# One transfer in place of two or three: x pieces, stage 2's load and its store in a Fourier mixing and routing kernel

## The chip, the cores and the metric

The kernel runs on one core of a Trainium2 chip. The metric is the device time of one execution in microseconds (us); a figure for a kernel is the median of several executions. All numbers below come from such executions, from one execution taken by the hardware profiler, or from the order of instructions in the built program.

A core has engines with instruction streams of their own: TensorE (PE in the profile, PEld for its weight loads), VectorE (DVE), ScalarE (ACT), GpSimd (POOL) and SyncE (SP), which computes nothing and here issues transfers. ACT and POOL issue transfers besides their computation. An engine takes its instructions in order, so one that waits holds up those behind it on that engine.

## The reference

The input is x with 8 batches of 2496 rows of 256 channels (float32). Each batch is filtered along its rows by a Fourier transform; then each of the 19968 rows goes through the two-layer network of one of 8 experts, which its token id selects.

```python
def _attn_ref(x, filt_r, filt_i):            # x (8, 2496, 256), filters (1249, 256)
    X = np.fft.rfft(x, axis=1)
    Y = X * (filt_r + 1j * filt_i)[None, :, :]
    return np.fft.irfft(Y, n=x.shape[1], axis=1).astype(np.float32)

def _moe_ref(x, token_ids, w1, w2):          # x (19968, 256), w1 (8, 256, 1024), w2 (8, 1024, 256)
    expert_idx = token_ids * np.int64(2654435761) % np.int64(8)
    out = np.zeros(x.shape, dtype=np.float32)
    for e in range(8):
        mask = expert_idx == e
        out[mask] = np.maximum(x[mask] @ w1[e], 0.0) @ w2[e]
    return out
```

## The kernel before

**The transform.** 2496 is written as N1 x N2 = 39 x 64: row s is 64 n1 + n2. Stage 1 (L238) multiplies by a 39-point transform over n1, for three values of n2 in one matmul; stage 2 (`forward`, L264) makes the 64-point transform, VectorE applies the filter, and `back` (L283) returns through 64 points; stage 3 (L365) returns through 39 and scatters the finished rows. The 39-point table `wf` has 117 rows: (n1, block of n2) in the order in which an x tile holds them. The 64 values of n2 lie in H = 3 blocks that begin at `H0 = (42, 0, 21)`.

**The transfers of the transform.** A batch's x comes in NV = 3 pieces of 8, 8 and 6 rows of each block (`load1`, L195). A piece is three DMAs, one for each block h (L205 to L209): each takes 39 rows of 8 KB (6 KB in the last piece) to every third partition, `xt[h:NR:H]`. All are issued by SP, apart from block 1 of batch 0, which ACT issues. Between stages 1 and 2 the rows go through a DRAM buffer d1 of shape (64, 40, 256): ACT stores (L254), SP loads (`load2`, L256) in 5 groups a batch, each as two DMAs of 64 partitions, one for each half p of the 40. Behind stage 2 the rows go through d2: ACT stores (L299) in 5 groups a batch, again as two DMAs, and SP loads them for stage 3 (`load4`, L360; "t<-d" in the profile), three a batch. Batches 0 and 1 skip d1 and d2 and turn their data on the chip with TensorE (`stage1_c`, `turn2`, `back_c`, `turn4`), so `load2` and the stores of `back` happen for six batches.

**The routing.** The scatters (POOL, L382) put each row, with its number, into the DRAM table xs, sorted by expert. xs is cut into NT = 85 tiles of TB = 256 rows, each of one expert. NSURE = 80 of them are always computed. The last five are conditional: three nested blocks, `rest(0)` to `rest(2)`, for tile 80, tile 81 and tiles 82 to 84, each entered only if the number of tiles in use, found on the chip, is larger.

**A tile's step** (`step`, L864). POOL forms differences of the weights for the next tile (L792) and scatters the previous tile's results (`store`, L844). `up` (L795) multiplies by w1 in seven block products of a Strassen-like scheme (`up_a`, `up_b`, `up_c`); VectorE adds their parts and ACT applies ReLU (L806). `down` (L832) multiplies by w2: 32 matmuls, `dps`. Within `up`, behind ACT's copy of L813, stands `load(i + 2)`: five DMAs on ACT (L762), four for the rows (`xg`) and one for the row numbers (`no`). Every ReLU of the tile stands behind these five in ACT's order. `weights(i + 2)` issues the next weights on SP (L413, L416), and skips the transfer where the expert stays the same. `token_parts` (L770) transposes a tile's rows on VectorE for the following tile.

**What sets the order.** The code is issued as written, with no scheduler behind it: `todo` (L697 to L736) is a list of pieces of the transform with hand-written due times, in units of tiles. Those due before 0 run ahead of tile 0, the others between and within the tiles' steps. Batches 2 to 7 are transformed beside the first 47 tiles.

**Semaphores of transfers.** In the built program every transfer that SP or ACT issues counts on one of eight semaphores. Both queues share these and take them in turn, in the order of the code. A transfer first waits until the previous transfer on its semaphore has landed. So a transfer of ACT can wait for one of SP, and which one depends on how many transfers lie between.

**The tail.** After tile 79 (L887 to L907), the rows of all five conditional tiles are transposed into `mid`, and the rows of tiles 82 to 84 are loaded, ahead of the first condition. Tiles 80 and 81 were loaded by the steps of tiles 78 and 79.

Of the kernel before, what the change touches and what calls it, by code (L numbers as in the profile page):

```python
# [19 lines left out]
P = 128  # L20
B, S, C = 8, 2496, 256
# [7 lines left out]
N1, N2 = 39, 64  # L29
NS, NQ = N1 // 2 + 1, 64  # L30
H, HN = 3, 21
H0 = (2 * HN, 0, HN)
NR = H * N1
NK = 2 * H * NS
SG = 4
XG = 4
NU = (HN + XG) // XG
XL = 2 * XG
# [5 lines left out]
NT = (N + E * (TB - 1)) // TB  # L44
# [8 lines left out]
NSURE = NT - 5  # L53
# [19 lines left out]
def dft_tables():  # L73
    n1 = np.arange(N1)
    n2 = np.array([H0[i % H] + i // H for i in range(N2)])
    s, q = np.arange(NS), np.arange(NQ)
    ph = 2 * np.pi * np.outer(n1, s) / N1
    w = np.stack([np.cos(ph), -np.sin(ph)], 1)
    wf = np.zeros((N1, H, H, 2, NS))
    wi = np.zeros((H, 2, NS, H, N1))  # L80
    v = np.stack([2 * np.cos(ph), -2 * np.sin(ph)], 0)
    v[0, :, 0], v[1, :, 0] = 1.0, 0.0
    for h in range(H):
        wf[:, h, h] = w
        wi[h, :, :, h] = v.transpose(0, 2, 1) / S

    kap = np.where(q[:, None] < 32, s + N1 * q[:, None], s + N1 * (95 - q[:, None]))
    sg = np.where(q < 32, 1.0, -1.0)[:, None]  # L90
    th = 2 * np.pi * ((n2[:, None, None] * kap) % S) / S
    c, sn = np.cos(th), np.sin(th)
    d = np.zeros((2, N2, NS, 2, NQ))
    d[0, :, :, 0] = c.transpose(0, 2, 1)
    d[1, :, :, 0] = sn.transpose(0, 2, 1)
    d[0, :, :, 1] = (-sn * sg).transpose(0, 2, 1)
    d[1, :, :, 1] = (c * sg).transpose(0, 2, 1)
    f32 = np.float32
    return (wf.reshape(NR, NK).astype(f32), wi.reshape(NK, NR).astype(f32),
            d.transpose(1, 0, 2, 3, 4).reshape(P, NS, P).astype(f32))  # L100
# [18 lines left out]
def kernel(  # L119
# [9 lines left out]
):  # L129
    nc = tc.nc  # L130
    wf_host, wi_host, d_host = dft_tables()
    wf_dram = nc.inline_tensor(wf_host, name="wf_tbl")
    wi_dram = nc.inline_tensor(wi_host, name="wi_tbl")
# [40 lines left out]
    def slot(kind):  # L174
        slots[kind].append(slots[kind].pop(0))
        return slots[kind][-1]
# [3 lines left out]
    class Batch:  # L180
# [14 lines left out]
        def load1(self, v):  # L195

            k = self.b * NV + v if self.b < 2 else NV + NV * (self.b > 2) + v
            if k <= NV:
                xt = wts[0:NR, k, :].rearrange("p (j c) -> p j c", c=C)
            else:  # L200
                xt = xpool.tile([NR, XL, C], F32, name=f"x_{self.b}_{v}", tag="x")
            self.x[v] = xt

            n = min(XL, HN + 1 - XL * v)
            for h in range(H):  # L205

                (nc.scalar if self.b == 0 and h == 1 else nc.sync).dma_start(out=xt[h:NR:H, 0:n, :],
                                  in_=bass.AP(tensor=x.tensor, offset=x.offset + (self.b * S + H0[h] + XL * v) * C,
                                              ap=[[N2 * C, N1], [C, n], [1, C]]))  # L209

        def products(self, w, rows, cols, src, dst, copy, u, name):

# [42 lines left out]

        def load2(self, g):  # L256
            t2 = slot("t2")
            for p in range(2):
                a0 = p * NS + SG * g
                nc.sync.dma_start(out=t2[p:P:2, :, :],  # L260
                                  in_=self.d1[:, a0:a0 + SG, :])
            self.t2[g] = t2

        def forward(self, u):  # L264
# [18 lines left out]
        def back(self, u):  # L283
            if self.d2 is None:
                self.d2 = dpool.tile([N2, 2 * NS, C], F32, name=f"d2_{self.b}", tag="d2")
            pr = self.p.pop(u)
            half = SG // 2
            if u % half == 0:
                self.g = slot("g")
            ps = fps.tile([P, 2, C], F32, name=f"pc_{self.b}_{u}", tag="f")  # L290
            for i in range(2):
                nc.tensor.matmul(out=ps[:, i, :], lhsT=e_t[:, 2 * u + i, :], rhs=pr[:, i, :],  # L292
                                 start=True, stop=True)
            i0 = 2 * (u % half)
            nc.scalar.copy(out=self.g[:, i0:i0 + 2, :], in_=ps[:])
            if u % half == half - 1:
                for p in range(2):
                    a0 = p * NS + SG * (u // half)
                    nc.scalar.dma_start(out=self.d2[:, a0:a0 + SG, :],  # L299
                                        in_=self.g[p:P:2, :, :])  # L300

# [449 lines left out]
    def load(i):  # L753

        g = gath.tile([P, TB // 32, C // 4], F32, name=f"xg_{i}", tag="xg")
        no = nums.tile([P, 2], I32, name=f"no_{i}", tag="no")
        rows = xs[tiles[i] * TB:(tiles[i] + 1) * TB, :]
        moves = [(g[32 * q:32 * q + 32, :, :], rows[:, 64 * q:64 * q + 64].rearrange("(a t) c -> t a c", t=32))
                 for q in range(4)]
        moves.append((no[:].bitcast(F32), rows[:, C:C + 1].rearrange("(h p) c -> p (h c)", p=P)))  # L760
        for to, src in moves:
            ld = (nc.sync if i < 2 else nc.scalar).dma_start(out=to, in_=src)  # L762
            for b in range(STAGES[stage_of[i]], B):
                tc.declare_no_dep(ld.ins, group=f"xs_{b}", reason="the tiles of a stage hold tokens of its batches alone")
            if stage_of[i] < G - 1:
                tc.declare_no_dep(ld.ins, group="xs_pad", reason="places without a token lie in the last stage alone")
            tc.add_to_no_dep_group("xs_read", ld.ins)
        xg[i], to_rows[i] = g, no

    def token_parts(i, to=None):  # L770

        xt = work.tile([P, DP, 2, P], F32, name=f"xt_{i}", tag="xt")[:] if to is None else to
        nc.vector.transpose(out=xt.rearrange("p d h (a t) -> p (h a) d t", t=32),  # L773
                            in_=xg[i][:, :, 0:C // 4].rearrange("p a (c d) -> p a d c", d=DP))
        parts[i] = {(h, d): xt[:, d, h, :] for h in range(2) for d in range(DP)}

    def token_sums(i):
        x = parts[i]
        st = work.tile([P, 4, P], F32, name=f"st_{i}", tag="st")
        for k, (p, q, op) in enumerate((((1, 0), (1, 1), OP.add), (0, (0, 0), OP.subtract),  # L780
                                        ((0, 0), (1, 0), OP.subtract), ((0, 1), 1, OP.subtract))):
            p, q = [st[:, v, :] if isinstance(v, int) else x[v] for v in (p, q)]
            nc.vector.tensor_tensor(st[:, k, :], p, q, op=op)  # L783
        parts[i]["sums"] = st

    def weight_sums(i, eng=None):

        eng, w1, h = eng or nc.gpsimd, ws[i][0], F // 2
        b11, b12, b21, b22 = [w1[:, d, f * h:f * h + h] for d in range(DP) for f in range(2)]
        t = [tpool.tile([P, h], F32, name=f"tw_{i}_{k}", tag=f"tw{k}") for k in range(4)]  # L790
        for k, (p, q) in enumerate(((b12, b11), (b22, t[0][:]), (b22, b12), (b21, t[1][:]))):
            eng.tensor_tensor(t[k][:], p, q, op=OP.subtract)  # L792
        sums[i] = t
# [38 lines left out]
    def down(i, ht, spot=lambda k: None):  # L832
        w2 = ws[i][1]
        ps = banks["d"].tile([P, 2, C], F32, name=f"dps_{i}", tag="d")
        for h in range(2):
            for fp in range(FP):
                nc.tensor.matmul(out=ps[:, h, :], lhsT=ht[:, h, fp, :], rhs=w2[:, fp, :],  # L837
                                 start=(fp == 0), stop=(fp == FP - 1))
                if fp % 4 == 3:
                    spot(2 * h + fp // 4)  # L840
        rows[i] = outs.tile([P, 2, C], F32, name=f"osb_{i}", tag="osb")
        nc.vector.tensor_copy(out=rows[i][:], in_=ps[:])  # L842
# [41 lines left out]
    assert not main  # L884
    store(NSURE - 1)

    for i in range(NSURE, NT):  # L887
        token_parts(i, mid[:, i - NSURE, 0:2 * TB].rearrange("p (d h t) -> p d h t", d=DP, h=2))
        if i + 2 < NT:
            load(i + 2)  # L890
    blocks = [range(NSURE, NSURE + 1), range(NSURE + 1, NSURE + 2), range(NSURE + 2, NT)]

    def rest(k):
        with tc.If(used[0] > blocks[k][0]):
            for i in blocks[k]:
                ht = work.tile([P, 2, FP, P], F32, name=f"ht_{i}", tag="ht")
                token_sums(i)
                weight_sums(i, nc.vector)
                up(i, ht)
                weights(i + 2, 0)  # L900
                down(i, ht)
                store(i)
                weights(i + 2, 1)
            if k + 1 < len(blocks):
                rest(k + 1)
# [29 lines left out]
```

## Time and profile before

| what | number | where from |
|---|---|---|
| executions | 1489.63, 1490.96, 1495.55 us | three runs; the median is 1490.96 |
| the profiled execution's own time | 1492.68 us | the profiled run |
| its span | 1490.9 us | from the first instruction of the profile to the last |
| PE busy | 1403.1 us, 94% of the span | busy time of the engines |
| DVE, POOL, ACT busy | 826.6 us (55%), 774.3 us (52%), 401.4 us (27%) | the same |
| DMA queue 1 (hardware) | 140.92 MB, 31.0% of 16 engines | queues |
| DMA queue 10 (hardware) | 58.59 MB, 16.0% | queues |
| DMA queue 0 (software: the scatters) | 44.59 MB, 8.7% | queues |
| granted TensorE clock | 0.977 of full speed, mean | the core's clock |

The span is what the profiler records; the device time of the same execution is 1.8 us longer. Busy time of an engine counts its instructions, without those that issue transfers or wait. These last have rows of their own, named after the engine's sequencer (SPq, ACTq, POOLq), and a long time in such a row is mostly a wait for a semaphore. A group's line gives the source line, engine and operation, output and input tiles with their sizes, and the count; behind the first bar stand the total busy time in us and the mean of one in ns, and behind the second the idle time of the engine just before, with what ended most of it. Letters such as `in_x_dram` are the program's names of tensors, without the numbers of buffers. A row of the timeline gives the start and the length in us, the engine, and what it ran. A row of a table by windows gives the window, its length, then for PE, weight loads, DVE, ACT, POOL and SP the busy time and the number of instructions, the mean granted clock, the mean busy share of the 16 DMA engines, and GB/s.

### The profile page before, as it was taken

Reading aid. Unit: us, or ns where it says so; the run is one execution under the profiler, and the core shown is the slowest. Engines: PE = TensorE matmul, PEld = TensorE weight load, DVE = VectorE, ACT = ScalarE, POOL = GpSimd, SP = SyncE. Lnnn points to the kernel's source line nnn. Section 1 sums busy time; section 2 is a strip of 40 time slices with the busy share of each in tenths; the row PEclk is TensorE's granted clock in tenths of the full one; section 3 lists DMA queues with packets and bytes.
Section 4 is the critical chain, followed back from the end, with each engine's and each line's share of the span. In section 5 each row is a group of like instructions: output and inputs, shape, how many; then the busy total and the mean of one; then the engine's idle time right before and its main releaser. Section 6 shows DMA issues by size and latency. Waiting matters only on the chain.

```text
span 1490.9 us, 24354 instructions
## 1 busy us (share of the span) xinstructions
PE 1403.1 (94%) x8746; PEld 1278.3 (86%) x8746; DVE 826.6 (55%) x1374; ACT 401.4 (27%) x710; POOL 774.3 (52%) x700
## 2 busy tenths in 40 slices
PE   5996699999999979999989999999999999999996
PEld 5985688888888868888978999998999999999996
DVE  6772565475556547544655466543555555656463
ACT  2563122222233212322222222222222222222221
POOL 5056332763475455567533566577564545464551
PEclk8998799999999989999999999999999999999998
DMA  8248567747988596888834763556523324241412
GB/s 213 48 137 256 146 198 185 228 152 245 275 235 259 163 272 217 254 268 265 255 115 120 197 192 100 158 148 206 156 72 97 97 63 124 71 127 44 147 35 54
DMA packets 234104, 245.70 MB, mean 165 GB/s; under 512 B 128604, under 2 KB 206351, under 8 KB 226861
## 3 DMA queue, kind: packets, MB, share of 16 engines
q1 hardware_dynamic: 77079, 140.92, 31.0%
q10 hardware_dynamic: 136982, 58.59, 16.0%
q0 software_dynamic: 19920, 44.59, 8.7%
q8 instruction: 72, 1.18, 0.3%
q14 instruction: 51, 0.42, 0.1%
HBM read 251.19 MB, written 75.14 MB: 219 GB/s over the span
## 4 chain that ended last, share of the span: by engine, by line
PE 63%; DMA 4%; ACTq 1%; DVE 0%; ACT 0%; issue 0%; DVEq 0%; SPq 0%
PE dps L837 30%; PE up_b L802 11%; PE up_a L802 7%; PE up_c L802 7%; PE pd L225 3%; PE pc L292 2%; DMA t<-d 2%; PE pb L269 2%; DMA xg<-xs 1%; ACTq L762 1%; PE pa L225 1%; ACT ht L806 0%; DMA out_dram<-osb,no 0%; PE pd L219 0%; DMA wts<-in_moe_w_dram 0%
## 5 line engine op out<-in xcount | busy, mean ns | idle before, releaser
L837 PE MATMUL dps<-wts,ht 128*128 128x256 f32 x2560 | 589.5, 384 | 24.9 <-ACT ht L806 24.9
L837 PEld LDWEIGHTS dps<-wts,ht 128*128 128x128 f32 x2560 | 487.2, 192 | 96.8 <-ACT ht L806 29.3
L792 POOL TENSOR_TENSOR tw<-wts 128x512 f32<-128x512 f32 x158 | 204.6, 1295 | 214.1 <-DMA wts<-in_moe_w_dram 164.2
L382 POOL DMA_INDIRECT xs<-o,sidx x176 | 176.2, 1001 | 194.3 <-ACT o L227 83.7
L809 DVE TENSOR_TENSOR ht<-up_b,ht 128x512 f32<-128x512 f32 x240 | 166.0, 691 | 175.9 <-PE up_b L802 165.1
L847 POOL DMA_INDIRECT out_dram<-osb,no x160 | 158.9, 993 | 198.5 <-DVE osb L842 165.6
L806 ACT ACTIVATE ht<-ht 128x512 f32<-128x512 f32 x240 | 148.9, 629 | 339.5 <-DMA xg<-xs 151.5
L792 POOL TENSOR_TENSOR tw<-wts,tw 128x512 f32<-128x512 f32 x158 | 206.1, 1304 | 6.2
L802 PE MATMUL up_a<-xt,wts 128*128 128x128 f32 x1280 | 183.4, 276 | 16.3 <-DVE xt L773 16.3
L842 DVE COPY osb<-dps 128x512 f32<-128x512 f32 x80 | 55.4, 692 | 257.6 <-PE dps L837 257.5
L802 PEld LDWEIGHTS up_a<-xt,wts 128*128 128x128 f32 x1280 | 169.0, 193 | 21.6 <-POOL tw L792 16.7
L802 PE MATMUL up_b<-st,tw 128*128 128x128 f32 x1280 | 170.6, 276 | 2.8 <-DVE ht L809 1.2
L802 PEld LDWEIGHTS up_b<-st,tw 128*128 128x128 f32 x1280 | 156.6, 193 | 4.2 <-issue 2.8
L813 ACT COPY ht<-up_a 128x512 f32<-128x512 f32 x80 | 46.9, 586 | 370.5 <-PE up_a L802 344.1
L809 DVE TENSOR_TENSOR ht<-up_c,ht 128x512 f32<-128x512 f32 x160 | 110.6, 691 | 62.1 <-PE up_c L802 52.6
L279 DVE TENSOR_TENSOR z<-pb,filt 64x512 f32<-64x512 f32 x160 | 110.1, 688 | 36.4 <-PE pc L292 34.5
L783 DVE TENSOR_TENSOR st<-xt 128x128 f32<-128x128 f32 x160 | 103.8, 649 | 2.8
L275 DVE TENSOR_TENSOR y<-pb,filt 128x512 f32<-128x512 f32 x80 | 55.1, 689 | 68.8 <-PE pb L269 66.9
L802 PE MATMUL up_c<-st,tw 128*128 128x128 f32 x640 | 85.2, 276 | 0.0
L802 PE MATMUL up_b<-xt,tw 128*128 128x128 f32 x640 | 84.5, 275 | 0.0
L802 PE MATMUL up_c<-st,wts 128*128 128x128 f32 x640 | 84.5, 275 | 0.0
L802 PEld LDWEIGHTS up_c<-st,tw 128*128 128x128 f32 x640 | 78.6, 194 | 0.0
(142 smaller groups left out, 1324.3 us busy)
## 6 DMA issues: line engine op xcount, KB each, us to landing
wts<-in_moe_w_dram SPq DMA_DIRECT2D x160, 1024.0 KB
xg<-xs ACTq DMA_DIRECT2D x332, 64.0 KB
mid<-d SPq DMA_DIRECT2D x60, 256.0 KB
d<-mid ACTq DMA_DIRECT2D x60, 256.0 KB
d<-mid ACTq DMA_DIRECT2D x12, 960.0 KB
t<-d SPq DMA_DIRECT2D x12, 960.0 KB
x<-in_x_dram SPq DMA_DIRECT2D x36, 312.0 KB
x<-in_x_dram SPq DMA_DIRECT2D x21, 234.0 KB
```

Source lines behind the costliest of these rows:

```text
L225: nc.tensor.matmul(out=ps[0:cols * H, k, :], lhsT=w[:], rhs=src[:, 2 * i + k, :], start=True, stop=True)
L275: nc.vector.tensor_tensor(out=y[:], in0=ps[:], in1=f_t[0][:, sl, :], op=OP.mult)
L279: nc.vector.tensor_tensor(out=z[b], in0=ps[a], in1=f_t[1][64 * hi:64 * hi + 64, s1:s1 + 2, :], op=OP.mult)
L382: st = nc.gpsimd.indirect_dma_start(out=xs[:], out_offset=bass.IndirectOffsetOnAxis(ap=index, axis=0), in_=rows, in_offset=None, bounds_ch ...
L783: nc.vector.tensor_tensor(st[:, k, :], p, q, op=op)
L792: eng.tensor_tensor(t[k][:], p, q, op=OP.subtract)
L802: nc.tensor.matmul(out=ps[bank][:, f, :], lhsT=w[:, f * P:(f + 1) * P], rhs=xx, start=first and f == 0, stop=True, skip_group_check=True)
L806: nc.scalar.activation(out=out, in_=in_, func=AF.Relu)
L809: nc.vector.tensor_tensor(out, ps[bank][:], other, op=OP.add)
L837: nc.tensor.matmul(out=ps[:, h, :], lhsT=ht[:, h, fp, :], rhs=w2[:, fp, :], start=(fp == 0), stop=(fp == FP - 1))
L842: nc.vector.tensor_copy(out=rows[i][:], in_=ps[:])
L847: st = nc.gpsimd.indirect_dma_start(out=out[:], out_offset=bass.IndirectOffsetOnAxis(ap=to_rows[i][:, h:h + 1], axis=0), in_=o[:, h, :], i ...
```

## The change

The change has four parts. The rows of `wf` are put in the order of the blocks in memory, so a piece of x is one DMA of 117 rows, always issued by SP. A group of `load2` is one DMA of 128 partitions, and so is a group of the store in `back`; the DRAM buffers are viewed as ((n p), s, c) for it. In the tail, only tiles 80 and 81 are transposed ahead of the first condition; the loads and the transposes of tiles 82 to 84 move into the third conditional block.

```diff
@@ dft_tables
     for h in range(H):
-        wf[:, h, h] = w
+        wf[:, H0[h] // HN, h] = w
         wi[h, :, :, h] = v.transpose(0, 2, 1) / S
@@ load1
             n = min(XL, HN + 1 - XL * v)
-            for h in range(H):
-
-                (nc.scalar if self.b == 0 and h == 1 else nc.sync).dma_start(out=xt[h:NR:H, 0:n, :],
-                                  in_=bass.AP(tensor=x.tensor, offset=x.offset + (self.b * S + H0[h] + XL * v) * C,
-                                              ap=[[N2 * C, N1], [C, n], [1, C]]))
+            nc.sync.dma_start(out=xt[:, 0:n, :],
+                              in_=bass.AP(tensor=x.tensor, offset=x.offset + (self.b * S + XL * v) * C,
+                                          ap=[[N2 * C, N1], [HN * C, H], [1, n * C]]))
@@ load2
             t2 = slot("t2")
-            for p in range(2):
-                a0 = p * NS + SG * g
-                nc.sync.dma_start(out=t2[p:P:2, :, :],
-                                  in_=self.d1[:, a0:a0 + SG, :])
+            nc.sync.dma_start(out=t2, in_=self.d1.rearrange("n (p s) c -> (n p) s c", p=2)[:, SG * g:SG * g + SG, :])
             self.t2[g] = t2
@@ back
             if u % half == half - 1:
-                for p in range(2):
-                    a0 = p * NS + SG * (u // half)
-                    nc.scalar.dma_start(out=self.d2[:, a0:a0 + SG, :],
-                                        in_=self.g[p:P:2, :, :])
+                a0 = SG * (u // half)
+                nc.scalar.dma_start(out=self.d2.rearrange("n (p s) c -> (n p) s c", p=2)[:, a0:a0 + SG, :], in_=self.g)
@@ the tail
-    for i in range(NSURE, NT):
+    for i in range(NSURE, NSURE + 2):
         token_parts(i, mid[:, i - NSURE, 0:2 * TB].rearrange("p (d h t) -> p d h t", d=DP, h=2))
-        if i + 2 < NT:
-            load(i + 2)
     blocks = [range(NSURE, NSURE + 1), range(NSURE + 1, NSURE + 2), range(NSURE + 2, NT)]
 
     def rest(k):
         with tc.If(used[0] > blocks[k][0]):
             for i in blocks[k]:
                 ht = work.tile([P, 2, FP, P], F32, name=f"ht_{i}", tag="ht")
+                if i >= NSURE + 2:
+                    for j in ((i, i + 1) if i == NSURE + 2 else (i + 1,)):
+                        if j < NT:
+                            load(j)
+                    token_parts(i)
                 token_sums(i)
                 weight_sums(i, nc.vector)
```

In the built program the two queues of SP and ACT hold 745 transfers in place of 853: 48 fewer for x, 30 for `load2` and 30 for the stores of `back`. The order of what remains is the same on every engine, apart from the three loads and three transposes that move into the condition. As the semaphores are taken in turn, almost every later transfer has another predecessor to wait for.

## The prediction

> **What bounds the kernel now.** I read the chain of waits first, then the costliest groups, then who PE waited for, then the timelines around PE's gaps. The chain's shares and two groups:
>
> ```profile
> PE 63%; DMA 4%; ACTq 1%; DVE 0%; ACT 0%; issue 0%; DVEq 0%; SPq 0%
> L837 PE MATMUL dps<-wts,ht 128*128 128x256 f32 x2560 | 589.5, 384 | 24.9 <-ACT ht L806 24.9
> L806 ACT ACTIVATE ht<-ht 128x512 f32<-128x512 f32 x240 | 148.9, 629 | 339.5 <-DMA xg<-xs 151.5
> ```
>
> TensorE leads: it is busy for 1403.1 of 1490.9 us, so at most 87.8 us can be won by better feeding. 2560 matmuls at 32 a tile are 80 tiles: none of the five conditional tiles ran. PE's waits (total, times, longest):
>
> ```profile
> PE dps L837 <- ACT ht L806: 24.9, 11, 8.7
> PE up_a L802 <- DVE xt L773: 16.3, 1, 16.3
> PE pa L315 <- DMA wts<-in_x_dram: 15.5, 2, 8.0
> PE pb L269 <- DMA mid<-d: 3.9, 1, 3.9
> ```
>
> The change can reach lines 1, 3 and 4, and the tail. The 16.3 us hang on the scatters of the first two batches and the first xg load behind them, which are not touched.
>
> Line 1 needs its mechanism. Each transfer that SP or ACT issues counts on one of eight semaphores that both queues share, and first waits for that semaphore's previous transfer. The chain near the longest gap (start, us, what):
>
> ```profile
> 518.90 16.12 DMA t<-d
> ...
> 535.04 0.38 ACTq L762
> ...
> 536.64 3.78 PE dps L837 x8
> ```
>
> ACT's fifth load of a tile's rows (L762) shares a semaphore with a t<-d load that takes 16.12 us. ReLU (1.12 us from 535.47) stands behind that load in ACT's order, so dps waits 8.70 us; the 8 matmuls after it take 3.78 us in place of 1.73, as the clock is low after a gap. From the timeline, gaps before dps are 2.88, 0.70, 0.89, 0.94, 2.80, 0.52, 8.70, 2.19, 0.85 and 4.18 us, at 258, 277, 295, 358, 411, 455, 537, 646, 666 and 774 us: tiles 6, 7, 8, 11, 14, 16, 20, 25, 26 and 32.
>
> **The change part by part.** 48 of 72 x transfers, 30 of 60 for stage 2's load and 30 of 60 for its store go: 108 of 853 on the two queues. Bytes stay.
>
> *Issue time.* An x piece takes 0.75 us of SP, a stage 2 load 0.58, a store 0.50 us of ACT (medians of their rows). The new forms are not in the trace; the nearest are 0.41 us (117 partitions, wf_t) and 0.34 us (128 partitions, w1). Per piece of work that is 3x0.75-0.41 = 1.8, 2x0.58-0.34 = 0.8 and 2x0.50-0.34 = 0.7 us, in all 24x1.8+30x0.8+30x0.7 = 88 us of sequencer time. I count it as 0: SP computes nothing, ACT is busy 27%. Without that cover a store's 0.7 us would be paid at most 30 times.
>
> [...]
>
> *Start.* PE waits for x at 8.03 and, 7.50 us, at 33.06 (batch 1's first piece). DMA engines are 0.95 to 1.11 busy from 8 to 24 us and 0.86 from 28 to 33, so bytes decide, and they are the same. Fewer semaphore waits let SP queue earlier: -1 us; ends +1 (one queue now carries the third that ACT carried) and -3.
>
> *First stage 2 load, 171.68 us.*
>
> ```profile
> 156.32 9.68 SPq L207 DMA_DIRECT2D x<-in_x_dram  x6
> 166.05 5.00 SPq L260 DMA_DIRECT2D mid<-d  x8
> ```
>
> SP needs 9.68 us for six issues because the fourth waits on a semaphore of tile 2's xg load (to 163.67). With two x transfers, no such wait stands ahead of the first stage 2 load. DMA was 0.62 to 0.69 busy from 156 to 168, so there is room: 1.87 MB of x, 0.5 MB of the load and 0.26 MB of rows at the 215 to 240 GB/s of busy stretches need 11 to 12 us plus about 2 of latency, 169.5 in place of 171.5. With the clock -2.3 us; ends 0 and -4.5.
>
> *Stalls of dps.* I took from the built program which transfer each new wait is for, and from this trace when that one landed. Tile 8 (0.89) and 11 (0.94): the predecessors are now old; -1.8, with the clock -2.3. Tile 32:
>
> ```profile
> 763.52 8.47 ACTq L762 DMA_DIRECT2D xg<-xs  x4
> ```
>
> These are the first four of the tile's five row loads. The fourth waited for the d store that ACT had issued at 763.07, to 771.66; it no longer does. Two of the four issues took 2.3 and 2.5 us without such a wait, and I keep those: ACT is through by 770, the gap falls from 4.18 to about 1.3, with 1.5 of clock -4.4 us; ends -2 and -6.2. Tiles 6, 7, 20, 25 and 26 keep the very same predecessors (t<-d); a store that lands a little sooner lets t<-d start sooner: -1 together. Tile 16: 0.
>
> Tile 14 is the loss. Its fifth load waited for a stage 2 load (to 408.96); it now waits for the second t<-d, issued at 396.44, for whose semaphore SP's next x piece waits to 416.11. SP, ACT, and the DMA engines in that stretch:
>
> ```profile
> 393.50 2.89 SPq L260 DMA_DIRECT2D mid<-d  x4
> 396.44 0.70 SPq L363 DMA_DIRECT2D t<-d  x1
> ...
> 416.11 2.47 SPq L207 DMA_DIRECT2D x<-in_x_dram  x3
> ```
>
> ```profile
> 409.48 0.63 ACT L806 ACTIVATE ht<-ht 128x512 f32<-128x512 f32 x1 [8.04 <-DMA xg<-xs]
> ```
>
> ```profile
> 400.00:410.00 10.00, 7.85 (x63) 7.23 (x62) 7.42 (x11) 1.10 (x2) 7.39 (x7) 1.00 1.06 286
> ```
>
> At 286 GB/s and a DMA share of 1.06 the queue is full, so two issues fewer ahead of t<-d bring it at most 1 us sooner: 415.4. The fifth load, issued at 409.05 in the trace, moves by 6.4 us, the gap grows from 2.80 to about 9.1; the clock's share, 3.21-1.73 = 1.5 before, becomes 2.05. +6.9 us; ends 0 (it lands by 409) and +9.
>
> *Conditional rows.* Three tiles' loads (15 issues on ACT, 1479.52 to 1486.9) and three transposes go; no conditional tile runs.
>
> ```profile
> 1484.48 1.91 ACTq L762 DMA_DIRECT2D xg<-xs  x4
> ...
> 1488.08 0.71 DVE L773 STREAM_TRANSPOSE mid<-xg 128x512 f32<-128x512 f32 x1 [1.88 <-DMA xg<-xs]
> L930 POOLq DRAIN  x3: 46/103/5132, 1484.9 to 1490.6; - x3
> ```
>
> The first two rows end at 1488.8 and look like the end. The last row is what is late next: POOL's drain at the program's end starts at 1484.90, as soon as the last store's semaphores are settled, lasts 5.13 us, to 1490.03, and the closing barrier follows. If 5.13 us is its own length, the end stays and only lighter traffic behind the stores counts: -0.4. If it only waits for the others, -5.0. Nothing that POOL does depends on the skipped loads, so I take -0.4.
>
> **Sum.** -1 -2.3 -2.3 -4.4 -1 +6.9 -0.4 = -4.5 us. The profiled execution took 1492.68 us (span 1490.9 and 1.8 around it), 1.7 above the median of 1490.96. Minus 4.5 is 1488.2 on its footing and **1486.5** on the median's, 0.3% less: within the 0.5% (7.5 us) below which a measurement of this kernel can't tell a change.
>
> **Rivals.**
> - *All that could go, goes*: 0.35. Either the drain is a wait (1486.5-4.6 = 1482), or t<-d of tile 14 lands by 409 (1486.5-6.9 = 1480). For it: the drain has no work that a row names. Against: POOL is behind every other engine at 1490.03, and the DMA engines are full around 410.
> - *Slower: ACT's wait on t<-d grows wherever it exists*: 0.16. Place: the fifth row load of tiles 6, 7, 14, 20, 25 and 26. With fewer semaphores held, SP runs further ahead, puts stage 2 and x bytes into full engines sooner, and t<-d and the rows take longer. Each us there is a us of PE, and low clock besides. Six tiles that lose 2.2 us each cost 13, more than the 4.5 won, and give 1500; from 0.75 us each it decides the sign. For it: tile 20's 16.12 us, a share of 1.05 from 520 to 536. Against: what SP issues behind t<-d stands behind it in its own queue too.
> - *The change doesn't do what it says*: 0.03. [...]
>
> **Numbers.** The summed case holds 0.46, with a range of its own from 1481 to 1493. With the rivals, 8 in 10 lie from 1476 to 1497. A part of the summed case crosses 1483.5: faster 0.40, same 0.42, slower 0.18.
>
> **What would show it.** PE's gap near 411 grows to about 9 us behind ACT's row load, that at 774 falls under 2, those at 295 and 358 vanish, that at 537 stays above 7; the wait of pb for mid<-d falls to about 2; POOL's last drain still takes about 5 us and ends last. I am wrong if the gap of tile 14 doesn't grow, if the drain shrinks, or if x loads land later than the sum of their pieces did.

## The result, and the profile after

| kernel | executions | median | range |
|---|---|---|---|
| before | 18 | 1490.89 us | 1481.63 to 1498.17 |
| after | 18 | 1491.17 us | 1486.91 to 1497.07 |

The ratio of after to before is 1.0007, with a 95% interval from 0.9990 to 1.0023. On 1490.9 us that is a change between -1.5 and +3.4 us: none that can be measured. The forecast was -4.5 us (1486.5); the time lies inside the range, but -4.5 lies outside the interval.

The profiled execution of after took 1491.27 us, its span is 1489.5. What PE waited for in it (line, releaser, then total, times and longest in us; L830 and L799 are the lines that were L837 and L806 before):

```profile
PE dps L830 <- ACT ht L799: 32.8, 10, 8.6
PE up_a L795 <- DVE xt L766: 15.9, 1, 15.9
PE pa L308 <- DMA wts<-in_x_dram: 14.1, 2, 8.1
PE pb L264 <- issue: 1.9, 1, 1.9
```

The wait of 3.9 us for stage 2's first load is gone from the list. The wait of dps for ReLU, which was 24.9 us, has grown to 32.8. So the merged transfers did remove waits, and as many others grew: the question is which, and why.

PE runs the same 8746 matmuls in the same order in both kernels, so each matmul's start in one profile can be set against its start in the other. Where the difference changes, time was won or lost. The table gives its change over stretches (cut at 157, 250, 290, 400, 440, 480, 700 and 810 us of before), beside the prediction's terms:

| stretch | predicted, us | profile pair, us | PE's gap there, before -> after, us |
|---|---|---|---|
| start, to tile 0's rows | -1 | -0.7 | 7.50 -> 5.97 (first piece of batch 1) |
| tile 2's rows, stage 2's first load | -2.3 | +0.1 | pb 3.92 -> 0; dps 0 -> 2.96 |
| tiles 6 and 7 | -0.4 | +1.5 | 2.88, 0.70 -> 4.04, 0.81 |
| tiles 8 and 11 | -2.3 | -2.2 | 0.89, 0.94 -> 0, 0 |
| tile 14 | +6.9 | +6.3 | 2.80 -> 8.39 |
| tile 16 | 0 | +2.5 | 0.52 -> 3.06 |
| tiles 20, 25, 26 | -0.6 | -2.5 | 8.70, 2.19, 0.85 -> 8.60, 2.02, 0.81 |
| tile 32 | -4.4 | -5.7 | 4.18 -> 1.80 |
| behind the last matmul | -0.4 | -0.7 | 12.74 -> 12.06 |
| sum | -4.5 | -1.4 | |

The prediction's -1 for five tiles is spread evenly here. A row's loss differs from its gaps by the low clock behind a gap (over the 6 us behind tile 14's gap the granted clock was 0.72 in before and 0.60 in after). The pair's -1.4 us is the difference of two single executions, of which before's lay 1.8 us above its median; the medians say 0. How far two profiles of one kernel can differ is seen in `after_again`, the kernel after profiled once more: its gaps are 4.26 us at tile 2 (2.96 here), 3.51 at tile 6, 8.28 at 14, 2.81 at 16, 10.05 at 20 and 1.89 at 32. A difference of a microsecond in one row can be chance; tiles 8, 11, 14, 16 and 32 came out alike.

Tile 14 in after, first ACT's timeline (start, length, engine and line, tiles, count; in square brackets the idle time before), then SP's:

```profile
399.59 1.61 ACTq L755 DMA_DIRECT2D xg<-xs  x3
...
413.26 0.39 ACTq L755 DMA_DIRECT2D no<-xs  x1
413.70 0.63 ACT L799 ACTIVATE ht<-ht 128x512 f32<-128x512 f32 x1 [13.63 <-DMA out_dram<-osb,no]
```

```profile
393.23 0.47 SPq L356 DMA_DIRECT2D t<-d  x1
398.53 4.12 SPq L409 DMA_DIRECT2D wts<-in_moe_w_dram  x1
```

The fifth row load (`no`) waits for the t<-d load issued at 393.23, whose last bytes land at 413.17, as its semaphore's events show. ReLU comes 0.4 us later, after 13.6 us of idle ACT. This is the loss that was forecast, in its place and nearly in its size.

At the end, the rows of the closing line:

```profile
L926 POOLq DRAIN  x3: 46/103/5132, 1483.5 to 1489.2; - x3
```

POOL's drain, an instruction of the program's end, lasts 5132 ns, to the nanosecond as before, though three tiles' loads and transposes are gone.

### The profile page after: what moved, and what is told of

It is laid out like the page before. It is cut to its first block, busy times and chain, and to the rows that moved or that the text cites. A ratio compares the mean times of both kernels' runs of the same rounds, so it can differ in the third digit from the quotient of the medians.

```text
span 1489.5 us, 24181 instructions
## 1 busy us (share of the span) xinstructions
PE 1400.7 (94%) x8746; PEld 1278.5 (86%) x8746; DVE 826.0 (55%) x1371; ACT 403.5 (27%) x710; POOL 774.3 (52%) x700
## 5 line engine op out<-in xcount | busy, mean ns | idle before, releaser
L830 PE MATMUL dps<-wts,ht 128*128 128x256 f32 x2560 | 586.0, 382 | 32.8 <-ACT ht L799 32.8
L830 PEld LDWEIGHTS dps<-wts,ht 128*128 128x128 f32 x2560 | 485.0, 191 | 103.0 <-ACT ht L799 36.2
L799 ACT ACTIVATE ht<-ht 128x512 f32<-128x512 f32 x240 | 149.8, 629 | 340.8 <-DVE ht L802 182.5
L806 ACT COPY ht<-up_a 128x512 f32<-128x512 f32 x80 | 46.9, 586 | 360.6 <-PE up_a L795 360.6
L274 DVE TENSOR_TENSOR z<-pb,filt 64x512 f32<-64x512 f32 x160 | 110.2, 689 | 34.7 <-PE pc L287 32.8
```

The costliest lines, as they stand in the source:

```text
L274: nc.vector.tensor_tensor(out=z[b], in0=ps[a], in1=f_t[1][64 * hi:64 * hi + 64, s1:s1 + 2, :], op=OP.mult)
L799: nc.scalar.activation(out=out, in_=in_, func=AF.Relu)
L806: nc.scalar.copy(out=h21, in_=ps["a"][:])
```

## The experiments

All ratios are to the kernel before in the same group of runs, with the 95% interval. In the second group (the four kernels from `after_late` to `x_store2_tail`) the kernel before itself took 1510.08 us, in the others 1490.54 and 1491.46, so between groups only ratios are compared. The groups ran on three different chips.

| run | ratio | median, us |
|---|---|---|
| x_only | 0.9916 (0.9895 to 0.9937) | 1480.29 |
| load2_only | 1.0054 (1.0037 to 1.0071) | 1498.67 |
| store2_only | 0.9913 (0.9893 to 0.9933) | 1478.24 |
| x31_late | 0.9976 (0.9957 to 0.9994) | 1486.95 |
| after_late | 0.9953 (0.9920 to 0.9987) | 1501.08 |
| before_late | 1.0009 (0.9988 to 1.0031) | 1512.60 |
| hold | 0.9989 (0.9971 to 1.0007) | 1509.05 |
| x_store2_tail | 0.9864 (0.9841 to 0.9887) | 1490.38 |
| after_again | 0.9987 (0.9970 to 1.0005) | 1489.59 |
| move_t4 | 0.9931 (0.9903 to 0.9958) | 1483.58 |
| tuned | 0.9868 (0.9842 to 0.9894) | 1473.24 |

### One part of the change at a time

The theory: the time is set by which earlier transfer each tile's row loads have to wait for, and a removed transfer changes that for the loads that follow it. The rival: each removed transfer saves a little, wherever it stands. Before these runs the predecessors (a transfer's predecessor is the one before it on its semaphore) were read from each built program, and the landing times from the trace of before.

`x_only` is the kernel before with the edits in `dft_tables` and `load1`.

> Only the pieces of x are merged (48 transfers fewer), the rest is as before. Theory 'which transfer a row load waits for': by the order of this kernel's transfers, the fifth row load of tile 8 waits 2.3 us after the first is issued in place of 4.4, that of tile 11 5.1 in place of 5.7, that of tile 16 8.0 in place of 6.7, and those of tile 32 no longer wait; 14 and 20 are as before. So PE's gaps near 295, 358 and 774 us go (0.9, 0.9, 4.2), the one near 455 grows from 0.5 to 1.8, with the start's -1.5 and 1.4 of low clock behind tile 32's gap: -8 us, 1483. Theory 'bytes sent sooner': as in the kernel after, a 3 us gap of dps near 169 us, which takes the place of pb's wait of 3.9 us near 171. Rival 'a fixed saving for each transfer': the gain of all parts in common is about 0, so this part is within 2 us of before and no gap moves by more than 1 us.

`load2_only` is the kernel before with the edit in `load2`.

> Only stage 2's loads are merged (30 transfers fewer). Theory 'which transfer a row load waits for': tile 14's fifth row load waits for the second t<-d load, 15.1 us after the first is issued in place of 8.0, tile 20's 13.6 in place of 12.0, tile 8's no longer; 32 is as before. PE's gap near 411 us grows from 2.8 to 9, that near 537 from 8.7 to 10.3, that near 295 (0.9) goes, that near 774 stays at 4.2: +7 us, 1498. Theory 'bytes sent sooner' alone: no gap near 169 us, since x_3_1 is still held by the fourth semaphore. Rival 'a fixed saving for each transfer': within 2 us of before.

`store2_only` is the kernel before with the edit in `back`.

> Only the stores behind stage 2 are merged (30 transfers fewer). Theory 'which transfer a row load waits for': tile 20's fifth row load waits 6.3 us after the first is issued in place of 12.0, those of tile 32 2.7 in place of 8.1; tile 14 is as before (8.0). PE's gap near 537 us falls from 8.7 to 3, that near 774 from 4.2 to under 0.5, that near 411 stays at 2.8: -5.7 -4.2 and about 2 of low clock, -11 us, 1479. Rival 'a fixed saving for each transfer': within 2 us of before.

Measured: 1480.3, 1498.7 and 1478.2 us where 1483, 1498 and 1479 were expected, and the rival has all three within 2 us of 1490.5. One part is 0.5% slower, two are 0.8 and 0.9% faster, as was expected from their predecessors. What PE waited for around tile 20 (between 520 and 545 us), in before, load2_only and store2_only:

```profile
PE dps L837 <- ACT ht L806: 8.7, 1, 8.7
```

```profile
PE dps L834 <- ACT ht L803: 11.2, 1, 11.2
```

```profile
PE dps L835 <- ACT ht L804: 4.1, 1, 4.1
```

The same tile with the same work waits 8.7, 11.2 or 4.1 us (expected 10.3 and 3). In six other profiles whose row load waits for the same transfer as in before, this gap is 8.6 to 10.1 us, so 4.1 lies far outside what chance does and 11.2 only just.

Misses: in x_only the gap of tile 14 fell too (2.80 to 1.03), that of tile 16 grew more than expected (0.52 to 3.61 in place of 1.8), tile 32 kept 1.5 us, and at tile 2 dps waited 1.4 us in place of 3. In store2_only tile 14's gap fell to 0.93 where 2.8 was expected, tile 32 kept 1.93 in place of under 0.5, and tile 25's grew from 2.19 to 4.09. The profiled execution of load2_only was its fastest, 1490 us; it shows tile 14's gap at 8.17 us and tile 20's at 11.24, but from tile 0's rows on it lost only 1.7 us against the profile of before, and its start was quicker. Its loss of 8 us is read from the nine timed executions; no profile shows where it arose.

The parts don't add up: -10.3 +8.1 -12.3 = -14.5 us, where all three with the tail give 0.

### Stage 2's load left as two transfers

`x_store2_tail` is the kernel after with the old `load2`:

```diff
-            nc.sync.dma_start(out=t2, in_=self.d1.rearrange("n (p s) c -> (n p) s c", p=2)[:, SG * g:SG * g + SG, :])
+            for p in range(2):
+                a0 = p * NS + SG * g
+                nc.sync.dma_start(out=t2[p:P:2, :, :],
+                                  in_=self.d1[:, a0:a0 + SG, :])
```

> The kernel after with stage 2's load left as two transfers (x pieces and stores merged, tail as after). Theory 'which transfer a row load waits for': tile 14 waits for a stage 2 load, 8.0 us after its first issue, as before; tile 20's wait is 6.3 in place of 12.0; those of tiles 8, 11, 21 and 32 are gone; tile 16's is 8.0 in place of 6.7. PE's gaps: 411 us at most 2.8, 455 us 2 to 3.5, 537 us about 3.5, 774 us under 2. With start, stage 2's first load and tail (-1.5, -2, -0.7): about -18 us, 1473, faster than before and after. Rival 'parts add up': the sum of the medians of x alone (-10.3) and stores alone (-12.3) is -22.6 and the tail -0.7, 1467. Rival 'it is chance in the landing times, and not the order': no nearer to 1473 than to 1491.

Measured: 0.9864, or 1470.6 us on 1490.9, between the 1473 of the theory and the 1467 of the rival that adds the parts; the interval, 1467.2 to 1474.0, hardly tells these two apart. Tile 16's gap, expected at 2 to 3.5 us, is gone, and tile 2's is 4.64. PE's waits of dps between 400 and 800 us, in this kernel and in after:

```profile
PE dps L833 <- ACT ht L802: 9.1, 5, 3.4
```

```profile
PE dps L830 <- ACT ht L799: 25.0, 7, 8.6
```

The kernel with 30 transfers more is 1.4% faster than after. So more transfers do not by themselves make this kernel slower.

### One exchange in SP's order

`move_t4` is the kernel after with one due time changed. In the built program two neighbours on SP change places, a t<-d load and the w2 weights behind it; nothing is added or removed.

```diff
-    todo += part3(3, spaced(12, 16, NU), [11.2, 11.4, 12.5])
+    todo += part3(3, spaced(12, 16, NU), [11.2, 11.8, 12.5])
```

`after_again` is the kernel after, as their base.

> The kernel after itself, as the base for the two others on the same chip: all theories expect a ratio to before within 0.998 and 1.004.

> The kernel after with one single exchange in SP's order: batch 3's second t<-d load is issued behind the w2 weights of that step in place of ahead of them. No transfer is added or taken away, and all other row loads wait for what they waited for. Theory 'which transfer a row load waits for': tile 14's fifth row load now waits for a stage 2 load that landed 7.5 us after the tile's first row load was issued, in place of 13.6; PE's gap near 415 us falls from 8.4 to about 2.3, with the low clock behind it -7 us, a ratio of 0.995 to the kernel after. Rival 'the DMA engines are full there, and the wait moves': another row load or stage 3 waits as long, and the ratio to the kernel after is 1.000.

Measured: 0.9931 to before, and 1483.58/1489.59 = 0.9960 to after, expected 0.995. PE's waits between 400 and 410 us in move_t4, where after has 8.4 us and after_again 8.3:

```profile
PE dps L830 <- ACT ht L799: 1.6, 1, 1.6
```

ACT's timeline there:

```profile
397.39 2.98 ACTq L755 DMA_DIRECT2D xg<-xs  x4
404.26 0.39 ACTq L755 DMA_DIRECT2D no<-xs  x1
404.69 0.63 ACT L799 ACTIVATE ht<-ht 128x512 f32<-128x512 f32 x1 [6.82 <-DMA xg<-xs]
```

The fifth load goes 6.9 us after the first, where it went 13.7 us after it in after. With the low clock behind the old gap, PE gained 9.0 us at this place in the profiles of this group; later tiles gave some back. That settles tile 14.

### Bytes sent sooner, at tile 2

The row loads of tile 2 wait for the same transfers as before, and yet dps now waits 3 us there. ACT's timeline in before, then ACT's and SP's in after:

```profile
158.09 1.97 ACTq L762 DMA_DIRECT2D xg<-xs  x4
161.89 0.38 ACTq L762 DMA_DIRECT2D no<-xs  x1
```

```profile
157.40 2.02 ACTq L755 DMA_DIRECT2D xg<-xs  x4
167.69 0.38 ACTq L755 DMA_DIRECT2D no<-xs  x1
```

```profile
155.39 1.77 SPq L205 DMA_DIRECT2D x<-in_x_dram  x2
157.21 12.11 SPq L256 DMA_DIRECT2D mid<-d  x4
```

The fifth load shares its semaphore with the first of the same tile, so it waits for that load's bytes. They land 3.8 us after issue in before and 10.3 us in after. In before the second x piece was held back to 163.67 (the prediction showed it as the delay of stage 2's load). In after both pieces, 1.9 MB, and a stage 2 load are issued ahead of the rows.

`x31_late` moves the second piece behind the four stage 2 loads.

```diff
-    todo += [(-75.3 + .1 * v, lambda v=v: batches[3].load1(v)) for v in range(2)]
+    todo += [(-75.3 + .8 * v, lambda v=v: batches[3].load1(v)) for v in range(2)]
```

> The kernel after, with the second x piece of batch 3 issued behind the four stage 2 loads of batch 2 in place of ahead of them; every later row load waits for the same transfer as in the kernel after. Theory 'bytes sent sooner': the 936 KB of that piece stood in the full DMA queues ahead of tile 2's rows, which landed 10.3 us after issue in place of 3.8; now they land about 4 us sooner, the 3 us gap of dps near 169 us goes, and with pb's wait still small the time is 1488, 3 us under the kernel after. Rival: tile 2's rows are late because of what each larger transfer does by itself, or stage 2's loads take the piece's place ahead of the rows: the gap stays at 3 us and the time at 1491. In both, the gaps near 415, 462 and 544 us stay at 8.4, 3.1 and 8.6.

The time came out near the expected one, 1486.95, but not for the reason given: the gap stayed, 3.01 us, as the rival said. A second stage 2 load took the piece's place ahead of the rows, which landed after 9.3 us. So this run doesn't show the theory, and its 0.3% is not explained by that gap.

`hold` moves the piece and three stage 2 loads behind the weights of tile 2, which SP can issue only when tile 0's products are done.

```diff
-    todo += [(-75 + .1 * g, lambda g=g: batches[2].load2(g)) for g in range(4)]
-    todo += [(-75.3 + .1 * v, lambda v=v: batches[3].load1(v)) for v in range(2)]
+    todo += [((-75, .11, .12, .13)[g], lambda g=g: batches[2].load2(g)) for g in range(4)]
+    todo += [((-75.3, .14)[v], lambda v=v: batches[3].load1(v)) for v in range(2)]
```

> The kernel after, with the second x piece of batch 3 and three of the four first stage 2 loads moved on SP behind the weights of tile 2, whose issue waits for tile 0's products; all later row loads wait for the same transfers as in the kernel after. Theory 'bytes sent sooner': only 1.4 MB are left ahead of tile 2's rows, they land about 5 us after issue in place of 10.3, and the gap of dps near 169 us (2.96) falls under 0.5; stage 2's first load is in time, so about 3.5 us less than the kernel after, 1487.5. Rival 'larger transfers are slow by themselves': the gap stays over 2 us. Rival 'the wait comes back at stage 2': the gap goes, but PE waits 3 us or more for mid<-d, and the time stays at 1491.

PE's waits between 150 and 185 us, all that there are:

```profile
PE up_a L795 <- DVE xt L766: 13.2, 1, 13.2
PE up_b L795 <- DVE tw L785: 1.0, 1, 1.0
PE up_b L795 <- issue: 0.2, 1, 0.2
```

The wait of dps is gone, and none for mid<-d has come. The rows landed after 6.5 us. The time's ratio is 0.9989 to after's 1.0007 and 0.9987, so 3 us can't be told from it; the gap can.

### ReLU out of the way of the loads

`after_late` and `before_late` issue a tile's five loads behind its last ReLU:

```diff
-        up(i, ht, lambda: load(i + 2) if i + 2 < NT else None)
+        up(i, ht)
+        if i + 2 < NT:
+            load(i + 2)
```

> The kernel after, with a tile's five row loads issued behind its last ReLU in place of ahead of the first. The loads still wait for other transfers, but no ReLU stands behind them. Theory 'ReLU behind a waiting load': the 32.8 us that dps waited for ReLU fall under 5 us; with up to 10 us of new waits (ACT's copies for the transform and the next tile's first copy now stand behind the loads) the time is 1455 to 1470. Rival 'the wait moves': the transform's copies are as urgent as ReLU, PE's waits for ACT copies grow by as much as dps wins, and the time is within 5 us of 1491.

> The kernel before, with the same move of the row loads behind the last ReLU. Theory 'ReLU behind a waiting load': the 24.9 us that dps waited for ReLU fall under 5 us, 1460 to 1475, and before and after with this move are within 5 us of each other, since the change acted on the time through those waits. Rival 'the wait moves': within 5 us of 1491. Rival 'the merged transfers are worth something by themselves': the kernel after with this move is over 8 us faster than this one.

The theory missed the size by far: 0.9953 and 1.0009, not some 0.98. What PE waited for in after_late, the lines that matter:

```profile
PE up_b L795 <- DVE ht L802: 7.5, 10, 1.6
PE pb L264 <- issue: 6.5, 3, 4.1
PE pd L223 <- ACT o L225: 4.9, 1, 4.9
...
PE up_a L795 <- ACT ht L806: 3.6, 1, 3.6
```

And what ACT waited for in it:

```profile
ACT mid L290 <- DMA xg<-xs: 20.2, 8, 6.5
ACT o L225 <- DMA wts<-in_moe_w_dram: 15.5, 2, 12.8
```

The wait of dps for ReLU is not among PE's waits of 0.7 us or more. But ACT's copies for stages 2 and 3 now stand behind the waiting loads, and PE waits there. PE's gaps sum to 70.1 us, against 77.8 in hold, a variant of after of the same group, and 68.6 in after in the first group. The wait moved, as the rival said. In before_late, PE also waits 10.3 us for stage 2's first load.

The third rival of before_late, that the merged transfers are worth something by themselves, came true in its number: after_late is 11.5 us faster than before_late in the same group, where it had said over 8. In the two profiles after_late is ahead by 3.7 us at 33 us, by 7.6 at 152, by 11.3 at 232 and by 9.3 at the last matmul, so the difference arises at the start and beside the first tiles. Part of it may be chance, since PE's gap before batch 1's first piece (6.4 us in before_late, 3.7 in after_late) varies as much between the other profiles. What the rest hangs on, the order or the count of transfers, was not tried.

### The order tuned by its predecessors

`tuned` is the kernel after with hold's edit, move_t4's, and three more shifts of due times:

```diff
-        out += part3(b, a3, [max(e0, a3[2 * v] - 2.2) for v in range(NV)])
+        out += part3(b, a3, [max(e0, a3[2 * v] - 2.2) + {(4, 1): -0.6, (5, 1): -0.3}.get((b, v), 0) for v in range(NV)])
-        out += part1(b, a1, [max(x0, a1[2 * v] - 2.5) for v in range(NV)])
+        out += part1(b, a1, [max(x0, a1[2 * v] - 2.5) + {(5, 2): 0.4}.get((b, v), 0) for v in range(NV)])
```

> The kernel after with only the order on SP changed: the hold of tile 2's run, the exchange at tile 14, and three shifts of due times (batch 4's second t<-d load 0.6 tiles earlier, batch 5's 0.3 earlier, batch 5's last x piece 0.4 later), after which the row loads of tiles 14, 16, 20 and 25 wait for transfers that land 7.5, 2.1, 6.6 and 0.7 us after the tile's first row load in place of 13.6, 9.3, 11.9 and 5.6. Theory 'which transfer a row load waits for': PE's gaps there fall to 2.3, 0, 3.3 and 0 and tile 2's 3 us go: -3.4 -7 -3.3 -5.5 -2 = -21 us, a ratio to the kernel after of 0.986, as good as the kernel with two loads in stage 2. Rival 'the wait moves': dps waits less, but stage 3 and the transform wait more, and the ratio to the kernel after is over 0.996.

Measured: 1473.24/1489.59 = 0.989 to after, 0.9868 to before: 16 us of the 21 expected. PE's waits over the whole run:

```profile
PE dps L830 <- ACT ht L799: 17.9, 8, 5.3
PE up_a L795 <- DVE xt L766: 15.9, 1, 15.9
PE pa L308 <- DMA wts<-in_x_dram: 12.2, 2, 8.0
```

dps waits 17.9 us in place of after_again's 34.1. The gaps of tiles 2 and 16 are gone, those of 14 and 20 are 1.4 and 5.3 us. Tile 25's did not go: it grew to 2.95. No transfer is larger or smaller than in after. `x_store2_tail` and `tuned` beat both kernels, by 1.4% and 1.3% of before.

## Why the prediction was right, and where its sum was off

**The mechanism held.** A ReLU behind a row load that waits on a shared semaphore was the thing that the change moved. move_t4 and the three single parts show it: each moved the time by about what was expected from the predecessors, with the bytes of every batch unchanged, if not gap by gap. It is not the whole of what merging does: after_late and before_late, without these waits, still differ by 11.5 us. The gaps at tiles 8 and 11 went, tile 32's fell under 2 us, tile 20's stayed above 7, and tile 14's grew to 8.4 as foretold (9.1).

**The drain was judged right.** That it waits for the others (the bound of -5.0 us) is refuted by the same 5132 ns after the loads went; what was won, 0.7 us, lies in front of it.

**Term "first stage 2 load, -2.3": its saving came, and tile 2 took it.** The wait of pb went entirely, 3.9 us, more than forecast. The step reckoned that there was room because the DMA engines were 0.62 to 0.69 busy, and asked only when stage 2's bytes would land. It did not ask whose bytes would land later: tile 2's rows, issued behind what SP now sends ahead of them. hold shows that. The 2 us of latency in its reckoning stand in the trace of before: the ten row loads that SP issues there from 151.4 to 155.8 us land 1.8 to 2.4 us after their issue.

**Term "tile 16: 0" should have been +2.5.** The transfers it could wait for were known, but their landing times were taken from the trace of before. Its fifth load now waits for batch 5's first d store (960 KB). ACT in after, then in before:

```profile
448.62 0.34 ACTq L252 DMA_DIRECT2D d<-mid  x1
...
451.55 4.36 ACTq L755 DMA_DIRECT2D xg<-xs  x4
460.87 0.38 ACTq L755 DMA_DIRECT2D no<-xs  x1
```

```profile
443.70 0.33 ACTq L254 DMA_DIRECT2D d<-mid  x1
...
446.70 5.85 ACTq L762 DMA_DIRECT2D xg<-xs  x4
453.40 0.38 ACTq L762 DMA_DIRECT2D no<-xs  x1
```

By its semaphore that store lands 12.2 us after issue in after and 8.5 us in before. The reason can be read from six kernels: where the x piece issued just ahead is three transfers, the store takes 8.5, 7.9 and 7.8 us (before, load2_only, store2_only); where it is one, 11.8, 11.4 and 12.2 (x_only, x_store2_tail, after). As one transfer, all 702 KB stand ahead of the store; as three, 234 KB did and the rest came behind it. That the bytes ahead are the cause is read from this order and was not tried alone. In tuned the one piece again stands just ahead and the store takes 11.0 us, yet the gap is gone: the row load waits there for the x piece, which lands in 6.3 us. So the gap hangs on which transfer is waited for.

**Term "tile 32, -4.4" was -5.7 by its clock.** The step reckoned 1.5 us of low clock. Six microseconds from just behind the gap, before (columns: window, its length, busy time of PE, weight loads, DVE, ACT and POOL with their counts, granted clock, DMA share, GB/s), then after:

```profile
774.00:780.00 6.00, 6.00 (x15) 4.74 (x16) 0.00 (x0) 1.28 (x3) 3.62 (x3) 0.51 0.21 62
```

```profile
776.30:782.30 6.00, 6.00 (x28) 5.30 (x29) 2.93 (x5) 1.57 (x3) 1.56 (x2) 1.00 0.60 199
```

The clock stood at 0.51 over these 6 us, 3 us lost, and behind the shorter gap at 1.00. The 4.18 us of gap cost 7 in all. In all thirteen profiles the granted clock is full or half, and the half starts on a grid of 3.41 us that runs through the profile. Between 170 and 1450 us, PE was idle for at least 1.76 us in each of the 48 full-clock windows that a half one followed, and for at most 1.94 in every one that a full one followed; in before and after alone these are 2.19 us, in eight windows, and 1.77. So the place of a gap on the grid counts: 2.19 us inside one window (tile 25, before) were followed by half clock, 3.06 us split over two (tile 16, after) were not. Tile 32's 4.18 us in before filled a window and reached 0.62 us into the next, and two half ones followed. Its 1.80 us in after cost no clock, nor did 1.89 us in after_again, but 1.90 us in x31_late did. The step took the clock's price from the eight matmuls behind tile 20's gap (3.78 us in place of 1.73); here it ran on for 6 us.

**Smaller terms.** Tile 14 was 0.6 us less than summed; its t<-d landed at 413.2 and not 415.4. Tile 6, one of five tiles for which -1 was allowed, lost 1.5: it waits for a t<-d load still. The start's -1 can't be judged: PE's gap before batch 1's first piece was between 3.7 and 7.5 us in the thirteen profiles, 4.2 us in load2_only, whose start is that of before. Most of what was won at tiles 20 to 26 is clock: tile 25's gap shrank by only 0.2 us, but lay inside one window in before and across two in after, worth 1.7 us. The bound of 87.8 us on better feeding leaves the clock out: 35 of the 1403 busy us in before ran at half.

**Issue time.** An x piece of 117 rows costs SP 0.92 us, not 0.41, a stage 2 load 0.44, not 0.34, a store 0.35 (medians). No wait in the profile goes back to it, so nothing speaks against counting it as hidden.

**A cost for each transfer.** The sum has none. With 108 transfers fewer the change is worth 0 (-1.5 to +3.4 us), and a kernel with 30 transfers more is faster than after by 1.4%. Even the 11.5 us between before_late and after_late would be 0.1 us for each. If a transfer has such a cost, it lay beside other work here. No row names the engines that a load of 117 rows uses; it leaves 14 updates on its semaphore, as a load of 39 rows does in before, where loads of 64 and 128 rows leave 16, so nothing shows that their count changed.

**The rivals.** "All that could go, goes" failed on both counts, the drain and tile 14. "Slower: ACT's wait on t<-d grows wherever it exists" grew at tiles 6 and 14 in this pair of profiles, and at 7 by 0.1 us; its mechanism, SP ahead with its bytes, was real at tile 2, and by the order at tile 16, where the wait is for other transfers. "The change doesn't do what it says" is out: the first piece of x comes as soon as before (PE starts at 8.09 us in place of 8.03).

So the step that failed in the sum is the landing times: predecessors were taken from the new program, but when these land was taken from the old trace. Tiles 2, 6 and 16 together are 6.8 us that the sum hadn't, and better results at 14, 20 to 26 and 32 gave back 3.8. That the total came so near is in part luck: errors of both signs made up for each other, and what the clock gave back at tiles 25 and 32 hung on where a gap fell on its grid.

The text ahead of the prediction says that transfers take the eight semaphores in turn. Mostly they do (the eleven that SP issues in before from 163.67 to 170.45 us count on 108, 100, 101, 102, 103, 104, 106, 107, 108, 100 and 101), but some are skipped in the built programs (tile 0's five row loads there count on 102, 104, 106, 108 and 101), so that a predecessor has to be read there and can't be counted.

## What to carry to other kernels

Where queues share a few semaphores in rotation, as SP and ACT share eight here, ask what a change in the number or order of transfers makes the later ones wait for: tile 14's fifth row load got a t<-d load in place of a stage 2 load as its predecessor, and PE's gap there went from 2.80 to 8.39 us. Read from the built program which waits now stand ahead of computing engines, before valuing the transfers themselves. The merged transfers also let SP run ahead and put their bytes in front of a small load that is urgent (tile 2's first row load landed after 10.3 us in place of 3.8), so look for what is issued just behind them. One exchanged pair won 6 us here where 108 transfers fewer won nothing. Moving the waiting instructions only moved the wait, since their new place has followers as urgent: PE's gaps sum to 70.1 us in after_late, and to 77.8 in hold and 68.6 in after.

## What the runs showed of the hardware that was not expected

- The drain on POOL at the program's end takes 5132 ns, the same to the nanosecond in all thirteen profiles, with and without the loads of tiles 82 to 84 in front of it.
- A load of 117 partitions with rows of 6 or 8 KB from a source of 39 by 3 takes 0.92 us of SP to issue (median), against 0.79 for one of the three with 39 rows that it replaces, and 0.44 for a load of 128 partitions with 4 KB.
- After a gap of 2.8 us (tile 14, before) the granted clock over the next 6 us was 0.72, after 4.2 us (tile 32) 0.51, after 8.4 us (tile 14, after) 0.60. The clock's price of a gap doesn't grow with its length in these; it hangs on how the gap lies on a grid of 3.41 us windows. Between 170 and 1450 us in the thirteen profiles, a full-clock window with over 1.94 us of idle PE was always followed by half clock, and one with under 1.76 never; the clock came back behind half windows with at most 0.42 us of idle, and not behind those with 0.62 or more.
- A store of 960 KB took 7.8 to 8.5 us where the load of 702 KB issued ahead of it was three transfers, of which two came behind the store (before, load2_only, store2_only), and 11.0 to 12.2 us where it was one (x_only, x_store2_tail, after, tuned).
